# Two attention layers with spectral layers between, one core: a key tile's two half units summed one behind the other, the first sums taken from key tiles 0 and 2, and two transfers moved

## The chip, the cores and the metric

The kernel runs on one core of a Trainium2 chip. The metric is the device time of one execution in microseconds, lower is better; three runs are given with their median. A profile of one further execution, with its own time, shows what each engine of the core did: TensorE (PE; its weight loads PEld), VectorE (DVE), ScalarE (ACT), GpSimd (POOL) and SyncE (SP), which here issues transfers and passes signals on.

## The reference

Four layers in a row on x of 2048 rows and 1024 columns, each added to its input: attention, spectral filter, attention, spectral filter. The change touches the attention alone.

```python
def _A_ref(x, wqkv, wo):                       # H = 32 heads of Dh = 32
    qkv = (x @ wqkv).reshape(B, S, 3, H, Dh).transpose(2, 0, 3, 1, 4)
    q, k, v = qkv[0], qkv[1], qkv[2]
    scores = jnp.einsum("bhqd,bhkd->bhqk", q, k) * (Dh ** -0.5)
    p = _softmax(scores, axis=-1)
    o = jnp.einsum("bhqk,bhkd->bhqd", p, v)
    return o.transpose(0, 2, 1, 3).reshape(B, S, D) @ wo
...
x = x + _A_ref(_layernorm(x, axis=-1), A_wqkv, A_wo)
x = x + _B_ref(_layernorm(x, axis=-1), B_w_r, B_w_i)
x = x + _A_ref(_layernorm(x, axis=-1), A_wqkv, A_wo)
x = x + _B_ref(_layernorm(x, axis=-1), B_w_r, B_w_i)
```

## The kernel before

**Groups, chunks, steps.** An attention layer works through 8 groups of 4 heads (`g`, line 854), and in each through 4 chunks of 512 queries (`c`). A chunk meets 16 key tiles of 128 keys (`kt`). In groups 0 to 6 `chunk` (line 817) does this in eleven steps, r = 0 to 10. Steps 0 to 9 call `S3` (line 701), which makes three units of scores of 128 x 1024 each: two for one whole key tile (halves 1 and 0, two heads each: `y` and `x`) and between them one for a half unit `z`: all four heads, but only one half (256) of the queries, of a second key tile. Two steps share that second tile: steps 2i and 2i+1 make the whole tiles 3i and 3i+2 and the two half units of tile 3i+1. Step 10 calls `S` (line 720) for tile 15. Each unit lies in one of three PSUM buffers. ScalarE turns it into exponentials (`exp`, line 695) in the order y, z, x, into a buffer of the pool `at_p`, which has 8 and goes round; a buffer is free again when both its users are done, the product with V and the sum.

**The users.** `PV` (line 731) multiplies the exponentials by V on TensorE; in the even steps it takes the last two steps' three key tiles. The softmax's denominators are made by adding the exponentials of all key tiles, element by element, into `acc` on VectorE: `add` (line 746) for a whole tile's half, `add_half` (line 755) for a half unit, which touches both halves of `acc` in 256 of 512 columns. The first sums of a chunk are written by a scalar_tensor_tensor of two exponentials, in place of a sum onto `acc`: in line 760 those of tiles 0 and 1, in four pieces of 512 columns; in group 7, which has no half units, in line 750. In step r the sums are those of step r-1's units: first half 1 of the whole tile, then the half unit, then half 0 (lines 841 to 846).

**The chunk's end.** In step 0 of the next chunk `boundary` (line 809) adds tile 15; `fin` (line 765) then has TensorE sum `acc` over the keys (L768: four matmuls for four heads, two on either half of `acc`, which run side by side), and VectorE makes and applies the reciprocals. `out` (line 781) splits the result in two f16 parts in step 2 (a cast on ScalarE, a subtraction on VectorE, L785), and `store` (line 778) writes them to `od` in DRAM in step 4.

**Work beside it.** In each odd step and in step 0 `slot` (line 800) puts 12 matmuls of the next groups' q, k or v on TensorE (L427, L472), into one PSUM bank. When a q or k bank is full, ScalarE casts it and VectorE writes the rest (`split`, L215 and L216). `norms` (line 441) uses that bank too, in steps 2, 6 or 10: four matmuls (L447) and a maximum on VectorE (L449). Weights come through SyncE (L300) into three stage buffers, each of which a split frees; two splits of 512 columns are made at a time.

**Group 6 to 7.** From chunk 2, step 7 of group 6 on, `slot` has matmuls of the output projection in place of q and k (`wo_parts`, line 579; L530). They read the head outputs of groups 0 to 6, which `load_o` (line 519) brings from `od` into the space of the normalised input: `load_o(0)` for queries 0 to 511, in two pieces, `load_o(1)` for the next 512. `xres` (line 533) loads rows of the residual, `load_wo` (line 501) the projection's weights.

**Order.** In groups 0 to 6 the order of TensorE, ScalarE and SyncE is that of the program (line 853); VectorE's is chosen by the framework's planner by its own modelled times, within the dependences. SyncE has a part in `S3` (lines 710 to 714): it waits for one matmul, and TensorE waits for SyncE before the last matmuls of the step. Whatever SyncE waits for or issues in between comes ahead of that.

Of the kernel before, what the change touches and what calls it, by code (L numbers as in the profile page):

```python
# [12 lines left out]
ALU = mybir.AluOpType  # L13
# [94 lines left out]
NG, NCH, NKT, NST = 8, 4, 16, 6  # L108
# [110 lines left out]
def run(g):  # L219
    for _ in g:  # L220
        pass
# [122 lines left out]
def attention(nc, tc, layer, ap, xin, yd, wts, wo, cst, dram, flags):  # L344
# [14 lines left out]
    def bank():  # L359

        if both:
            both.append(True)
            if len(both) % 2:
                return psO.tile([128, 512], F32, name="o")
        return psX.tile([128, 512], F32, name="x")
# [75 lines left out]
    def norms(z=None):  # L441
        kind, g = ph = left_norms.pop(0)
        if g not in mx:
            mx[g] = sm.tile([128, 2], F32, name="mqk")
        z = psS.tile([128, 2, 512], F32, name="s")[:, 0] if z is None else z
        for c in range(4):
            nc.tensor.matmul(z[32 * c:32 * c + 32], cst["bones"], nrm[ph][:, c], start=True, stop=True)  # L447
        i = 0 if kind == "k" else 1
        nc.vector.reduce_max(mx[g][:, i:i + 1], z, axis=AX.X)  # L449
        if kind == "q":  # L450
            mkbias(g)
# [67 lines left out]
    def load_o(c):  # L519
        osb[c] = xhl[:, 2 + c % 2]  # L520
        for i in range(2):
            nc.sync.dma_start(osb[c][:, i, 0:7], od[i, 0:7, :, c * 512:(c + 1) * 512].rearrange("g p n -> p g n"))
# [21 lines left out]
    def wo_part(c, t, dst, nd):  # L544

        x = xres(c, t)
        st = sm.tile([128, 2, 6], F32, name="st")
        for n in range(2):
            p = bank()
            m = wo_mm(p, c, t, n, range(nd))  # L550
            for _ in range(3 * nd - 1):
                next(m)
                yield
            run(m)
            sl = slice(n * 512, n * 512 + 512)
            nc.vector.scalar_tensor_tensor(dst[:, sl], p, 1.0 / (SO * SW), x[:, sl], op0=ALU.mult, op1=ALU.add)
            if nd == 8:
                nc.vector.bn_stats(st[:, n], dst[:, sl])
                if n:
                    r0 = c * 512 + t * 128  # L560
                    nc.sync.dma_start(yd[r0:r0 + 128, :], dst)
                    nc.vector.bn_aggr(mvs[:, 8 * c + 2 * t:8 * c + 2 * t + 2], st)
            yield
# [13 lines left out]
    wo_dst = [ap.x[:, 10 + t if t in SPILL else t] for t in range(8)] + [None] * 2 + [ap.x[:, t] for t in (10, 11)]  # L577

    def wo_parts():
        load_o(0)  # L580
        load_o(1)
        for t in (2, 3, 0, 1, 4, 5, 6, 7, 8, 9, 10, 11):
            if t == 8:
                two = wvp.tile([128, 2, 1024], F32, name="wv")
                wo_dst[8], wo_dst[9] = two[:, 0], two[:, 1]
            yield from wo_part(t // 4, t % 4, wo_dst[t], 8 if t == 11 else 7)
            if t in (1, 7):
                load_o(t // 4 + 2)
# [104 lines left out]
    P, Z, O, acc = {}, {}, {}, ap.acc  # L693
# [7 lines left out]
    def S3(g, c, kt, kz, qh):  # L701

        y, z, x = (psS.tile([128, 2, 512], F32, name="s") for _ in range(3))
        zv = z.rearrange("p j (s q) -> p j s q", q=256)
        for h, i, half in RUN:
            r, (a, b) = slice(32 * h, 32 * h + 32), TERMS[i]
            o, k, q, n = ((zv[:, h % 2, h // 2], kz, c * 512 + 256 * qh, 256) if half else
                          ((x, y)[h // 2][:, h % 2], kt, c * 512, 512))
            m = nc.tensor.matmul(o, K[g][r, a, k * 128:k * 128 + 128], Q[g][r, b, q:q + n], start=i == 0, stop=i == 2).ins  # L709
            if (h, i, half) == (1, 2, 1):  # L710
                turn = nc.sync.nop(nofuse=True).ins  # L711
                tc.add_manual_dep(turn, m.name, sync, reason="the first row tiles are done with the bank")
            if (h, i, half) == (2, 0, 1):
                tc.add_manual_dep(m, turn.name, sync, reason="the last row tiles follow in the same bank")
        P[g, c, kt, 1] = exp(g, pp.tile([128, 2, 512], F32, name="p"), y)
        p = exp(g, pp.tile([128, 2, 512], F32, name="p"), z)
        Z[g, c, kz, qh] = p.rearrange("p j (s q) -> p s j q", q=256)
        P[g, c, kt, 0] = exp(g, pp.tile([128, 2, 512], F32, name="p"), x)

    def S(g, c, kt):  # L720

        s = [psS.tile([128, 2, 512], F32, name="s") for _ in range(2)]
        for i, (a, b) in enumerate(TERMS):
            for h in range(4):
                r = slice(32 * h, 32 * h + 32)
                nc.tensor.matmul(s[h // 2][:, h % 2], K[g][r, a, kt * 128:kt * 128 + 128],  # L726
                                 Q[g][r, b, c * 512:c * 512 + 512], start=i == 0, stop=i == 2)
        for hf in range(2):
            P[g, c, kt, hf] = exp(g, pp.tile([128, 2, 512], F32, name="p"), s[hf])

    def PV(g, c, kt):
        if kt == 0:
            O[g, c] = psO.tile([128, 512], F32, name="o")
        parts = [(slice(256 * q, 256 * q + 256), Z[g, c, kt, q]) for q in range(2)] if (g, c, kt, 0) in Z else \
            [(slice(0, 512), [P[g, c, kt, hf] for hf in range(2)])]
        for q, p in parts:
            for h in range(4):
                r = slice(32 * h, 32 * h + 32)
                src = p[:, h // 2, h % 2] if len(parts) == 2 else p[h // 2][:, h % 2]
                nc.tensor.matmul(O[g, c][r, q], V[g][:, kt, r], src, start=kt == 0, stop=kt == NKT - 1)  # L740
        if kt == NKT - 1:
            o = ap.oc.tile([128, 512], F32, name="oc")
            nc.scalar.copy(o, O[g, c])
            O[g, c] = o

    def add(g, c, kt, halves=(0, 1)):
        for hf in halves:
            p = P[g, c, kt, hf]
            if kt == 1:
                nc.vector.scalar_tensor_tensor(acc[:, hf], P[g, c, 0, hf], 1e-34, p, op0=ALU.add, op1=ALU.add)  # L750
            elif kt:
                last_add = nc.vector.tensor_add(acc[:, hf], acc[:, hf], p)  # L752
        return last_add if kt > 1 else None

    def add_half(g, c, kt, q):

        sl = slice(256 * q, 256 * q + 256)
        if kt == 1:
            for hf in (1, 0):
                nc.vector.scalar_tensor_tensor(acc[:, hf, :, sl], P[g, c, 0, hf][:, :, sl], 1e-34, Z[g, c, kt, q][:, hf],  # L760
                                               op0=ALU.add, op1=ALU.add)
        else:
            nc.vector.tensor_add(acc[:, :, :, sl], acc[:, :, :, sl], Z[g, c, kt, q])  # L763

    def fin(g, c, z):
        zt = on.tile([128, 16, 32], F32, name="zt")
# [26 lines left out]
    pend, done, stores = [], [], []  # L793
# [15 lines left out]
    def boundary(w):  # L809

        last_add = add(*w)
        with tc.issue_after(last_add.ins):
            wts.look()
        done.append(w[:2])
        fin(*w[:2], psS.tile([128, 2, 512], F32, name="s")[:, 0])

    def chunk(g, c):

        for r in range(11):
            i, b = divmod(r, 2)  # L820
            n = 6 * c + (r + 1) // 2
            if r < 10:
                S3(g, c, 3 * i + 2 * b, 3 * i + 1, b)
            else:
                S(g, c, 15)
            if g == c == r == 0:
                run(last_v)
            if r and not b:
                for k in range(3):
                    PV(g, c, 3 * i - 3 + k)  # L830
                    if k == 1 and r in (2, 6, 10):
                        while left_norms:
                            norms(bank())
            if r == 0 and pend:
                PV(*pend[0])
                boundary(pend.pop())
            if r == 2 and done:
                stores.append(out(*done.pop(), store=False))
            if r == 4 and stores:
                store(*stores.pop())  # L840
            if r:
                i, k = divmod(r - 1, 2)
                if r > 2:
                    add(g, c, 3 * i + 2 * k, (1,))
                add_half(g, c, 3 * i + 1, k)
                add(g, c, 3 * i + 2 * k, (0,) if r > 2 else (1, 0))
            if b or r == 0:
                slot(g, n)
            if g == NG - 2 and 4 <= n + (b or r == 0) and left and (left.pop(0) % 3 < 2):
                next(lwo)  # L850
        pend.append((g, c, 15))
# [5 lines left out]
    g = NG - 1  # L857
    with tc.manual_schedule(engines={mybir.EngineType.PE, mybir.EngineType.Activation}):
        for u in range(NCH * NKT):
            c, kt = divmod(u, NKT)  # L860
# [587 lines left out]
```

## Time and profile before

| what | us |
| --- | --- |
| median of 3 runs | 3869.43 |
| the runs | 3868.97 to 3872.74 |
| the profiled execution | 3873.68 |
| its span, first to last instruction | 3871.7 |
| TensorE busy (mean granted clock 0.99) | 3695.9 |
| VectorE busy | 3237.9 |
| ScalarE busy | 2926.3 |

In a row of the timeline stand the start and the duration in us, the engine, the line of the kernel, the operation, what it writes and reads, partitions x elements, and how many such instructions follow one another without a pause; brackets give the idle time of the engine before it and what ended that. A row of waits gives who waited for what, the total in us, how often, and the longest. A row by lines gives the busy time, the mean of one in ns, and the idle time before them. Two instructions of VectorE may overlap by some 0.08 us.

### The profile page before, as it was taken

Reading aid. Unit: us, or ns where it says so; the run is one execution under the profiler, and the core shown is the slowest. Engines: PE = TensorE matmul, PEld = TensorE weight load, DVE = VectorE, ACT = ScalarE, POOL = GpSimd, SP = SyncE. Lnnn points to the kernel's source line nnn. Section 1 sums busy time; section 2 is a strip of 40 time slices with the busy share of each in tenths; the row PEclk is TensorE's granted clock in tenths of the full one; section 3 lists DMA queues with packets and bytes.
Section 4 is the critical chain, followed back from the end, with each engine's and each line's share of the span. In section 5 each row is a group of like instructions: output and inputs, shape, how many; then the busy total and the mean of one; then the engine's idle time right before and its main releaser. Section 6 shows DMA issues by size and latency. Waiting matters only on the chain.

```text
span 3871.7 us, 90485 instructions
## 1 busy us (share of the span) xinstructions
PE 3695.9 (95%) x38871; PEld 1923.6 (50%) x38871; DVE 3237.9 (84%) x3890; ACT 2926.3 (76%) x3683; POOL 289.0 (7%) x388
## 2 busy tenths in 40 slices
PE   8999999999999899999999999999999998999998
PEld 5434544454455333368964345434543543333788
DVE  6798999899989888985658899989998998789754
ACT  5787888888888766668748888878887877666586
POOL 1000000000000000014410000000000000000143
PEclk9999999999999999999999999999999999999999
DMA  6000000000000211233150010010001102111333
GB/s 180 15 12 23 7 18 16 20 15 12 20 21 21 78 55 63 77 126 115 56 147 31 23 34 26 23 31 26 19 23 34 34 29 77 56 66 72 148 98 106
DMA packets 150156, 199.09 MB, mean 51 GB/s; under 512 B 58224, under 2 KB 104048, under 8 KB 148720
## 3 DMA queue, kind: packets, MB, share of 16 engines
q1 hardware_dynamic: 148416, 192.62, 15.5%
q8 instruction: 306, 5.01, 0.5%
q14 instruction: 106, 0.87, 0.1%
q10 hardware_dynamic: 1328, 0.59, 0.1%
HBM read 132.35 MB, written 48.23 MB: 47 GB/s over the span
## 4 chain that ended last, share of the span: by engine, by line


## 5 line engine op out<-in xcount | busy, mean ns | idle before, releaser
L696 ACT ACTIVATE p<-s,bias 128x1024 f32<-128x1024 f32 x2048 | 2138.8, 1111 | 657.0 <-PE s L709 427.9
L752 DVE TENSOR_TENSOR R<-R,p 128x1024 f32<-128x1024 f32 x1344 | 1595.5, 1220 | 105.0 <-ACT p L696 59.3
L740 PE MATMUL o<-p,R 128*32 128x512 f32 (+1 forms) x10432 | 980.5, 510 | 0.0
L427 PE MATMUL x<-big,wqk 128*128 128x512 f16 x2880 | 661.7, 380 | 16.8 <-DVE mqk L449 14.5
L709 PEld LDWEIGHTS <-R 32*128 32x128 f16 x13440 | 380.3, 92 | 503.7 <-issue 361.3
L763 DVE TENSOR_TENSOR R<-R,p 128x1024 f32<-128x1024 f32 x448 | 549.0, 1226 | 50.5 <-ACT p L696 3.5
L740 PEld LDWEIGHTS o<-p,R 128*32 128x32 f32 x10432 | 300.8, 110 | 420.2 <-issue 327.2
L427 PEld LDWEIGHTS <-wqk 128*128 128x128 f16 x3072 | 283.9, 98 | 406.3 <-issue 97.3
L709 PE MATMUL s<-R 32*128 32x512 f16 (+1 forms) x7680 | 389.1, 323 | 12.2 <-SPq L711 7.9
L472 PE MATMUL x<-wv,big 128*128 128x256 f16 x2784 | 326.7, 275 | 11.9 <-DVE mqk L449 8.0
L472 PEld LDWEIGHTS <-big 128*128 128x128 f16 x3072 | 293.5, 98 | 82.2 <-issue 40.5
L709 PE MATMUL s<-Q,R 32*128 32x512 f16 (+1 forms) x5760 | 285.6, 325 | 25.2 <-SPq L711 25.0
L530 PE MATMUL x<-big 128*128 128x512 f16 x1050 | 245.2, 384 | 11.7 <-DMA big<-od 11.7
L760 DVE SCALAR_TENSOR_TENSOR R<-p 128x512 f32<-128x512 f32 x224 | 145.3, 669 | 119.2 <-ACT p L696 119.2
L530 PEld LDWEIGHTS <-big 128*128 128x128 f16 x1344 | 125.2, 98 | 188.9 <-issue 38.6
L455 POOL PARTITION_ALL_REDUCE mall<-mqk x16 | 13.7, 855 | 2359.8 <-DVE mqk L449 2348.4
L1110 DVE TENSOR_TENSOR H<-G,H 128x512 f16<-128x512 f32 (+1 forms) x68 | 47.0, 692 | 120.2 <-ACT H L1109 120.0
L726 PE MATMUL s<-Q,R 32*128 32x512 f16 x1824 | 125.6, 377 | 2.7 <-DVE R L571 2.7
L1055 ACT COPY U<-ps 64x256 f32<-64x256 f32 (+1 forms) x272 | 97.0, 357 | 8.4 <-PE ps L1062 3.1
L726 PEld LDWEIGHTS <-R 32*128 32x128 f16 x2208 | 41.1, 92 | 124.9 <-issue 104.1
L768 PE MATMUL s<-R,ones 128*32 128x512 f32 x512 | 87.7, 609 | 14.3 <-DVE R L752 9.7
L1062 PE MATMUL ps<-cbi,H 128*128 128x256 f16 (+1 forms) x792 | 98.6, 273 | 2.8 <-ACT H L1109 1.8
(448 smaller groups left out, 3307.0 us busy)
## 6 DMA issues: line engine op xcount, KB each, us to landing
wst<-in_wp SPq DMA_DIRECT2D x96, 256.0 KB, 2.9
R<-y SPq DMA_DIRECT2D x32, 512.0 KB, 5.3
w<-in_w SPq DMA_DIRECT2D x60, 256.0 KB, 2.7
od<-ohl SPq DMA_DIRECT2D x56, 256.0 KB, 2.4
big<-od SPq DMA_DIRECT2D x16, 896.0 KB, 6.7
y<-R SPq DMA_DIRECT2D x20, 512.0 KB, 2.8
wst<-in_wo SPq DMA_DIRECT2D x32, 256.0 KB, 2.6
xres<-in_x SPq DMA_DIRECT2D x16, 512.0 KB, 3.9
```

What stands on the lines that cost most here:

```text
L427: nc.tensor.matmul(ps, a, b, start=i == 0, stop=i == 23)
L472: nc.tensor.matmul(ps[:, j], x[c][:, d, o:o + 128], w[:, n, d], start=i == 0, stop=i == 23)
L530: nc.tensor.matmul(p, a, b, start=start and d == ds[0] and i == 0, stop=stop and d == ds[-1] and i == 2)
L696: nc.scalar.activation(p, s, AF.Exp, bias=bias[g], scale=SCALE / (SQ * SQ))
L709: m = nc.tensor.matmul(o, K[g][r, a, k * 128:k * 128 + 128], Q[g][r, b, q:q + n], start=i == 0, stop=i == 2).ins
L726: nc.tensor.matmul(s[h // 2][:, h % 2], K[g][r, a, kt * 128:kt * 128 + 128], Q[g][r, b, c * 512:c * 512 + 512], start=i == 0, stop=i == 2)
L740: nc.tensor.matmul(O[g, c][r, q], V[g][:, kt, r], src, start=kt == 0, stop=kt == NKT - 1)
L752: last_add = nc.vector.tensor_add(acc[:, hf], acc[:, hf], p)
L760: nc.vector.scalar_tensor_tensor(acc[:, hf, :, sl], P[g, c, 0, hf][:, :, sl], 1e-34, Z[g, c, kt, q][:, hf], op0=ALU.add, op1=ALU.add)
L763: nc.vector.tensor_add(acc[:, :, :, sl], acc[:, :, :, sl], Z[g, c, kt, q])
L1055: nc.scalar.copy(ov[64 * r:64 * r + 64, a0:a0 + m, x], tl[64 * x:64 * x + 64, :m, r])
L1062: nc.tensor.matmul(out, l, r, start=k == 0, stop=k == len(mm_) - 1)
```

## The change

Four things change, all in `attention`.

- The order of the sums. In odd steps from 3 on only the whole tile of the step before is summed, both halves. In even steps the two half units of tile 3i-2 are summed one behind the other, then both halves of tile 3i-1. In step 1 nothing is summed.
- The first sums: tiles 0 and 2, in two instructions of 1024 columns in step 2, and tile 1's half units are then added as any other's. Group 7 keeps tiles 0 and 1.
- `store` stands in step 6 of the next chunk, not in step 4.
- `load_o(0)` stands in step 1 of chunk 2 of group 6, not at the start of `wo_parts` (step 7 of that chunk).

```diff
     def wo_parts():
-        load_o(0)
         load_o(1)
...
             p = P[g, c, kt, hf]
-            if kt == 1:
+            if kt == (1 if g == NG - 1 else 2):
                 nc.vector.scalar_tensor_tensor(acc[:, hf], P[g, c, 0, hf], 1e-34, p, op0=ALU.add, op1=ALU.add)
             elif kt:
                 last_add = nc.vector.tensor_add(acc[:, hf], acc[:, hf], p)
-        return last_add if kt > 1 else None
+        return last_add if kt > 2 else None
...
         sl = slice(256 * q, 256 * q + 256)
-        if kt == 1:
-            for hf in (1, 0):
-                nc.vector.scalar_tensor_tensor(acc[:, hf, :, sl], P[g, c, 0, hf][:, :, sl], 1e-34, Z[g, c, kt, q][:, hf],
-                                               op0=ALU.add, op1=ALU.add)
-        else:
-            nc.vector.tensor_add(acc[:, :, :, sl], acc[:, :, :, sl], Z[g, c, kt, q])
+        nc.vector.tensor_add(acc[:, :, :, sl], acc[:, :, :, sl], Z[g, c, kt, q])
...
-            if r == 4 and stores:
+            if r == 6 and stores:
                 store(*stores.pop())
-            if r:
-                i, k = divmod(r - 1, 2)
+            if b and r > 1:
+                add(g, c, 3 * i, (1, 0))
+            elif r and not b:
+                if r == 2:
+                    add(g, c, 2, (1, 0))
+                for k in range(2):
+                    add_half(g, c, 3 * i - 2, k)
                 if r > 2:
-                    add(g, c, 3 * i + 2 * k, (1,))
-                add_half(g, c, 3 * i + 1, k)
-                add(g, c, 3 * i + 2 * k, (0,) if r > 2 else (1, 0))
+                    add(g, c, 3 * i - 1, (1, 0))
+            if (g, c, r) == (NG - 2, 2, 1):
+                load_o(0)
             if b or r == 0:
                 slot(g, n)
```

## The prediction

> **What bounds the kernel now.** First the busy times in the two stretches in which the change lies, attention groups 0 to 6 of either layer (columns: PE, PEld, DVE, ACT and POOL busy, clock, DMA share, GB/s).
>
> ```profile
> 109.00:1407.00 1298.00, 1243.99 (x14570) 580.49 (x14569) 1169.12 (x1202) 1056.96 (x1164) 24.41 (x28) 0.99 0.07 22
> ...
> 2032.00:3334.00 1302.00, 1247.36 (x14586) 580.44 (x14585) 1177.09 (x1214) 1057.48 (x1164) 24.83 (x28) 0.99 0.10 32
> ```
>
> TensorE sets the end: it idles 54.0 us in the first stretch and 54.6 in the second. VectorE is busy for 1169 of 1298 us, 90%, beside it. What this change can win lies in those 109 us, and in matmuls that run slowly after a pause. So the next view is what TensorE waits for (total, times, longest).
>
> ```profile
> PE s L709 <- SPq L711: 32.9, 12, 4.2
> PE x L447 <- DVE R L216: 17.0, 6, 2.8
> PE x L427 <- DVE mqk L449: 14.5, 14, 1.3
> PE x L530 <- DMA big<-od: 11.7, 4, 4.3
> PE x L447 <- DVE Q L216: 11.5, 8, 1.6
> ...
> PE s L768 <- DVE R L752: 9.7, 8, 1.7
> ...
> PE x L472 <- DVE mqk L449: 8.0, 6, 1.6
> ...
> PE x L427 <- DVE R L216: 1.9, 6, 0.6
> ```
>
> All but the transfer are VectorE being late. L447 and L427 want a PSUM bank that a split (L216) or a maximum (L449) on VectorE has still to read. In the first row SyncE stands behind a weight load whose buffer VectorE's split has to free, and TensorE waits for the signal that SyncE passes on in every `S3`. For a sum itself (L752, L763) only `fin` (L768) waits; the sums matter because VectorE does its work in order, so whatever stands behind them comes when they are done.
>
> **The pace of the sums.** A chunk with little other work: VectorE, then TensorE and ScalarE in the same stretch.
>
> ```profile
> 440.36 1.29 DVE L760 SCALAR_TENSOR_TENSOR R<-p 128x512 f32<-128x512 f32 x2 [2.13 <-ACT p L696]
> 441.57 3.49 DVE L752 TENSOR_TENSOR R<-R,p 128x1024 f32<-128x1024 f32 x3
> ...
> 450.89 2.36 DVE L752 TENSOR_TENSOR R<-R,p 128x1024 f32<-128x1024 f32 x2
> 453.36 1.23 DVE L763 TENSOR_TENSOR R<-R,p 128x1024 f32<-128x1024 f32 x1
> 454.69 2.36 DVE L752 TENSOR_TENSOR R<-R,p 128x1024 f32<-128x1024 f32 x2
> ...
> 441.15 1.16 PE L709 MATMUL s<-Q,R 32*128 32x256 f16 x24
> ...
> 444.96 1.15 PE L709 MATMUL s<-Q,R 32*128 32x256 f16 x24
> ...
> 438.21 3.12 ACT L696 ACTIVATE p<-s,bias 128x1024 f32<-128x1024 f32 x3 [2.43 <-PE s L709]
> ```
>
> TensorE takes 444.96 - 441.15 = 3.81 a step, VectorE 454.69 - 450.89 = 3.80 for three sums: once late, it stays late. Two L752 of different halves follow at 2.36 - 1.22 = 1.14; into and out of a half unit's sum (L763), which reads both halves, the pitch is (3.80 - 1.14) / 2 = 1.33: a dependent sum costs 0.19 more. Now two steps hold two pitches of 1.14 and four of 1.33, 7.60. After the change they hold the order 3i (both halves), the two half units, 3i+2 (both halves): four of 1.14 and two of 1.33, 7.22, **0.38 less for two steps**, if the second half unit (other columns) need not wait for the first. The nearest rows: two writes to interleaved columns of one tile follow without a wait.
>
> ```profile
> 1657.57 0.68 DVE L195 TENSOR_TENSOR R<-xn 128x512 f32<-128x512 f32 x1
> 1658.17 0.69 DVE L194 TENSOR_TENSOR R<-xn 128x512 f32<-128x512 f32 x1
> ...
> L750 DVE SCALAR_TENSOR_TENSOR R<-p 128x1024 f32<-128x1024 f32 x16 | 18.8, 1218 | 0.0
> ```
>
> They start 0.60 apart with 0.68 of duration. I take no wait; the other end is 0.19 per pair of half units.
>
> **The start costs.** Four L760 (two take 1.29) become two wide ones of 1.218 (L750's row): 0.2 less work, but later. The first needs step 1's first exponential (438.21 + 1.11 = 439.32), the second its third (441.33): 441.36 to 442.59, then the half units (0.10 after it, then 1.14) to 445.07. Before, 441.57 + 3.49 = 445.06 saw one sum more done. So the new order is one pitch, **1.14, behind** after step 2; 0.76 after step 4, 0.38 after 6, level after 8, and 0.38 ahead at the last sums. The buffers of `p` are held longer: the first exponential of step 3 (445.8) takes the one that the first half unit frees at 443.9, 1.9 of cover.
>
> **The waits, by that ledger.** Rows of the kinds that count:
>
> ```profile
> 522.92 2.10 PE L768 MATMUL s<-R,ones 128*32 128x512 f32 x8 [1.41 <-DVE R L752]
> 524.95 2.76 PE L427 MATMUL x<-big,wqk 128*128 128x512 f16 x12
> ...
> 663.44 1.06 PE L768 MATMUL s<-R,ones 128*32 128x512 f32 x8
> 664.44 2.76 PE L427 MATMUL x<-big,wqk 128*128 128x512 f16 x12
> ...
> 537.21 0.68 DVE L449 TENSOR_REDUCE mqk<-x 128x1 f32<-128x512 f32 x1
> ...
> 705.06 3.12 ACT L696 ACTIVATE p<-s,bias 128x1024 f32<-128x1024 f32 x3 [2.35 <-PE s L709]
> ...
> 710.61 2.35 DVE L752 TENSOR_TENSOR R<-R,p 128x1024 f32<-128x1024 f32 x2
> 713.49 1.06 PE L768 MATMUL s<-R,ones 128*32 128x512 f32 x8
> ```
>
> `fin` takes 664.44 - 663.44 = 1.00 where the sums are in time and 2.03 where they are late (its two pairs then run one behind the other). Over one turn of two groups (eight chunks) the boundaries at 433, 477, 523 and 569 are late: four in eight, 28 in all, x -0.38 = -10.6. Where VectorE had caught up, its last sum ends at 710.61 + 2.35 = 712.96, ahead of the `fin` at 713.49. There step 9's second exponential (705.06 + 2.1 = 707.2) is now followed by its half unit, two sums, a split and the last two sums: 1.33 + 1.14 + 1.14 + 0.60 + 1.14 + 1.23, to 713.8, 0.3 past TensorE; two in eight, 14 x 0.3 = +4.2. The splits of step 10 (6 waits): -0.38 x 6 = -2.3. Those of step 6 (8 + 6 waits): +0.38 x 14 = +5.3. The maximum L449 at 537.21 came behind the sums up to the first half unit of kt 4; now behind the two wide ones, a split, two halves and one sum, from 531.66: 537.05, -0.16 x 20 = -3.2. SyncE's weight load (step 8) is level: 0. **Sum -7.** This assumes that the planner, which orders VectorE, puts the other work behind as many finished exponentials as now.
>
> **The earlier load.** Layer one, then two; last SyncE's issues.
>
> ```profile
> 1342.30 1.15 PE L709 MATMUL s<-R 32*128 32x256 f16 x24
> 1347.72 0.60 PE L530 MATMUL x<-big 128*128 128x512 f16 x2 [4.27 <-DMA big<-od]
> 1350.13 4.02 PE L530 MATMUL x<-big 128*128 128x512 f16 x9 [1.81 <-DMA big<-od]
> ...
> 1358.48 1.16 PE L709 MATMUL s<-R 32*128 32x256 f16 x24
> ...
> 1367.35 1.06 PE L768 MATMUL s<-R,ones 128*32 128x512 f32 x8
> ...
> 3269.17 1.16 PE L709 MATMUL s<-R 32*128 32x256 f16 x24
> ...
> 3280.72 1.15 PE L709 MATMUL s<-R 32*128 32x256 f16 x24
> ...
> 1342.90 4.24 SPq L522 DMA_DIRECT2D big<-od  x4
> ...
> 1347.19 2.33 SPq L539 DMA_DIRECT2D xres<-in_x  x1
> ...
> 1356.69 1.23 DVE L752 TENSOR_TENSOR R<-R,p 128x1024 f32<-128x1024 f32 x1 [6.45 <-ACT p L696]
> ...
> 1363.57 3.69 DVE L752 TENSOR_TENSOR R<-R,p 128x1024 f32<-128x1024 f32 x3
> ```
>
> Two steps took 16.18 in place of 7.62, one 11.55 in place of 3.81: 8.56 + 7.74 = 16.3 lost, gaps and slow matmuls (0.43 each at 1350.13, 0.23 at 524.95). Six steps (23 us) earlier the data is there long before: the second piece's mark came 1350.13 - 1342.90 = 7.2 after the first issue. Both ends of the copy allow it: the last reader of the space is in the chunk before, and the stores that it reads were issued a chunk earlier. SyncE's issues: four take 4.24, so two some 1 to 2, between turns 3.81 apart; at the old place the other two and `xres` (2.33) just fit, and cost up to 2 if not. The weight loads queued behind have over two steps of cover. But the pause also let VectorE catch up (6.45 idle): 1356.69 less 6.45 is 1350.24, and the chunk's rest took 1363.57 + 3.69 - 1356.69 = 10.57. Without the pause it ends at 1360.8, while `fin`, 8.56 earlier than its 1367.4, would be due at 1358.8: 2.0 late, of which the new order takes 0.4; so 1.6 of each layer goes back there, 3.2 in all. **Sum -13.** The store two steps later costs nothing: its subtraction has long finished, and the tile has a second buffer.
>
> **Rivals.** (1) *The planner packs finer*: with the sums bunched, other VectorE work slips in one sum earlier (at most 1.14 each): step 10 6.8, step 6 11, weight loads 6.8, L449 22, together 46, half of it 23: 3803 to 3826. For: a tie between a sum and a split is decided by small modelled times. Against: now a split always stands behind the third exponential's sum. (2) *The load's gain is given back* (VectorE's backlog, SyncE's issues): 3 instead of 13, and the sums 0: 3866. (3) *The pace does not rise, slower*: the second half unit waits for the first. Then two steps give 0.19, step 2 leaves 1.33, and the last sums are 0.57 late: `fin` 28 x 0.57 + 4, step 10 3.4, step 6 14 x 0.95, weight loads 6 x 0.76: +41, less 13: 3898. It decides once two steps give less than 1.14 / 4 = 0.28. Against: L194 and L195.
>
> The Trainium skill (VectorE: DVE Perf Modes, "The DRAIN you can't avoid") says that a semaphore between chained operations costs nothing extra. By that rule the pace stays, and rival 3 is dearer (1.14 late at every `fin`, some 3920). The trace disagrees, 1.33 against 1.14, so it gets 0.02 of rival 3's chance.
>
> **How the numbers follow.** The execution profiled took 3873.7 (span 3871.7), 4.3 above the median 3869.4. 3873.7 - 7 - 13 = 3853.7, at the median's level **3849**. Chances: forecast 0.50 (own range 3837 to 3861), rival 1 0.20, rival 2 0.13, rival 3 0.17. The range 3815 to 3882 leaves out the end of rival 1 and most of rival 3. A measurement tells some 0.2% (7.7 us) from no change: faster 0.68, same 0.17, slower 0.15.
>
> **What would show it.** Two L763 1.14 apart (1.33: rival 3). L530's wait for the load gone, the two steps near 3.8. The gap before step 2's sums about 2 and then 0.9. `fin` nearer 1.0 at half the boundaries. L447's longest 2.8 at 2.4, or under 1.7 for rival 1; the 4.2 of SyncE unchanged, or near 3. What makes it wrong: an exponential that waits for a sum, which no row shows now.

## The result, and the profile after

The kernel after takes 3835.39 us (median of 4 runs, 3834.0 to 3837.64) where the kernel before took 3869.2 (4 runs): a ratio of 0.9912, 95% interval 0.9895 to 0.9929, so 0.9% faster. The forecast was 3849, its range 3815 to 3882. The execution profiled took 3834.0 (span 3832.0). One of the six executions of load_alone, a run of the next section, was in a slow state (4497.39); its time there is the median of the other five.

The waits of TensorE in the profile after (who waited for what, total, times, longest; S3 is now L708, `fin` L762, whole sums L751, half units L757):

```profile
PE x L427 <- DVE mqk L449: 27.6, 14, 2.2
PE s L708 <- SPq L710: 16.1, 8, 2.5
PE x L472 <- DVE mqk L449: 13.2, 6, 2.2
...
PE s L762 <- DVE R L751: 6.3, 8, 1.4
...
PE x L447 <- DVE R L216: 5.2, 6, 0.9
...
PE x L530 <- DVE mqk L449: 2.8, 2, 1.6
...
PE x L447 <- DVE Q L216: 1.0, 6, 0.2
```

Beside the rows of before: the wait for the transfer is gone, SyncE's 32.9 has become 16.1 and the splits' 28.5 (L447) 6.2; but the maximum, 22.5 before, now costs 43.6. The gain is the small difference of two large changes, and a forecast that is near in sum can be wrong in both.

A second view puts sizes on it. The page has no table by step, so this one is worked out from the trace: from the first score matmul of a step to that of the next, added over the 56 chunks of groups 0 to 6 of both layers, in us against the kernel before. It holds the runs of the next section too. Each row is one execution, and that of the kernel before was 4.3 above its median, so one or two us in a column mean nothing.

```
                 step 0   step 3   step 6   step 7   step 8  9, 10    all
after              -4.7    +22.3    -12.3     -6.9    -16.9  -16.7  -33.0
load_alone         +0.3     -0.4     +0.8    -14.2     -1.3   -1.6  -16.8
sums_alone         -5.3    +23.8    -12.4     +5.1    -15.3  -16.8  -20.7
before_split       -1.6     -0.1    -10.1     +6.3     -9.5  -13.3  -28.5
before_max        +31.1    -18.6     +4.2     +0.1     -0.4   +2.0  +18.1
before_all        +38.8    -18.6     -4.8    -21.1    -18.3  -13.2  -36.2
mixed_split       +15.2    +19.1     -6.8     -5.3     -8.4   -4.6   +8.6
after_mixed       +21.2    +25.7     +7.7     -5.4     +7.7   +3.2  +59.7
after_max          +5.3    -18.7     -8.6    -21.2    -15.1  -16.8  -74.1
after_start       -12.6     -2.8    -14.4     -7.6    -24.3  -23.1  -85.1
```

Step 0 holds the ones sums (`fin`), steps 3 and 7 what follows a maximum, steps 6, 8, 9 and 10 what waits for a split (step 8: for SyncE, which stands behind a weight load and so behind a split). The late transfer lay in steps 7 and 8 of one chunk in each layer. Steps 1, 2, 4 and 5 are left out; "all" holds them.

VectorE's timeline shows how one kernel can lose at step 3 and win at step 6. First the start of a chunk after (start, duration; in brackets the idle time before and what ended it), then TensorE at the same place:

```profile
524.25 1.23 DVE L749 SCALAR_TENSOR_TENSOR R<-p 128x1024 f32<-128x1024 f32 x1 [1.97 <-ACT p L695]
526.26 1.23 DVE L749 SCALAR_TENSOR_TENSOR R<-p 128x1024 f32<-128x1024 f32 x1 [0.78 <-ACT p L695]
527.40 0.69 DVE L216 SCALAR_TENSOR_TENSOR R<-x,R 128x512 f16<-128x512 f32 x1
528.00 2.35 DVE L757 TENSOR_TENSOR R<-R,p 128x1024 f32<-128x1024 f32 x2
530.46 2.36 DVE L751 TENSOR_TENSOR R<-R,p 128x1024 f32<-128x1024 f32 x2
532.74 0.68 DVE L449 TENSOR_REDUCE mqk<-x 128x1 f32<-128x512 f32 x1
```

```profile
528.85 0.40 PE L447 MATMUL x<-sq,bones 128*32 128x512 bf16 x4
...
530.03 1.24 PE L708 MATMUL s<-R 32*128 32x256 f16 x24
533.48 0.81 PE L427 MATMUL x<-big,wqk 128*128 128x512 f16 x3 [2.21 <-DVE mqk L449]
```

The two half units take 2.35 together, so they start 2.35 - 1.22 = 1.13 apart: the second does not wait for the first. But VectorE idles 1.97 and 0.78 before the two wide first sums, and the maximum, whose four matmuls are done at 529.3, stands behind two half units and both sums of key tile 3. TensorE waits 2.21 for it, where the kernel before waited 1.27 at the same place:

```profile
537.95 2.75 PE L427 MATMUL x<-big,wqk 128*128 128x512 f16 x12 [1.27 <-DVE mqk L449]
```

A later stretch of a chunk after shows the pace and the split's place:

```profile
674.37 4.63 DVE L751 TENSOR_TENSOR R<-R,p 128x1024 f32<-128x1024 f32 x4
679.03 2.36 DVE L757 TENSOR_TENSOR R<-R,p 128x1024 f32<-128x1024 f32 x2
681.43 1.23 DVE L751 TENSOR_TENSOR R<-R,p 128x1024 f32<-128x1024 f32 x1
682.57 0.68 DVE L216 SCALAR_TENSOR_TENSOR R<-x,R 128x512 f16<-128x512 f32 x1
```

Two steps' sums take 681.43 - 674.37 = 7.06, against 7.60 before; and the split stands behind the first half's sum of its step, ahead of the second's. The kernel before in the same chunk:

```profile
687.54 1.23 DVE L763 TENSOR_TENSOR R<-R,p 128x1024 f32<-128x1024 f32 x1
688.87 1.23 DVE L752 TENSOR_TENSOR R<-R,p 128x1024 f32<-128x1024 f32 x1
690.01 0.68 DVE L216 SCALAR_TENSOR_TENSOR R<-x,R 128x512 f16<-128x512 f32 x1
```

Here the split stands behind the second half's sum (688.87) as well: in the kernel after the planner has put it one sum earlier.

### The profile page after: what moved, and what is told of

The parts are those of the page before. It is cut to its first block, busy times and chain, and to the rows that moved or that the text cites. A ratio compares the mean times of both kernels' runs of the same rounds, so it can differ in the third digit from the quotient of the medians.

```text
span 3832.0 us, 89965 instructions
## 1 busy us (share of the span) xinstructions
PE 3694.9 (96%) x38871; PEld 1924.6 (50%) x38871; DVE 3222.6 (84%) x3778; ACT 2927.7 (76%) x3683; POOL 289.3 (8%) x388
## 4 chain that ended last, share of the span: by engine, by line
## 5 line engine op out<-in xcount | busy, mean ns | idle before, releaser
L751 DVE TENSOR_TENSOR R<-R,p 128x1024 f32<-128x1024 f32 x1232 | 1450.2, 1220 | 76.0 <-ACT p L695 54.3
L427 PE MATMUL x<-big,wqk 128*128 128x512 f16 x2880 | 668.7, 383 | 28.1 <-DVE mqk L449 27.6
L757 DVE TENSOR_TENSOR R<-R,p 128x1024 f32<-128x1024 f32 x560 | 666.3, 1221 | 31.8 <-ACT p L695 25.2
L708 PEld LDWEIGHTS <-R 32*128 32x128 f16 x13440 | 379.6, 92 | 487.9 <-issue 364.9
L708 PE MATMUL s<-R 32*128 32x512 f16 (+1 forms) x7680 | 389.7, 323 | 7.7 <-ACT p L695 5.3
L708 PE MATMUL s<-Q,R 32*128 32x256 f16 (+1 forms) x5760 | 282.8, 323 | 14.9 <-SPq L710 14.7
L749 DVE SCALAR_TENSOR_TENSOR R<-p 128x1024 f32<-128x1024 f32 x128 | 156.1, 1225 | 158.6 <-ACT p L695 158.6
L530 PE MATMUL x<-big 128*128 128x512 f16 x1050 | 240.8, 380 | 2.8 <-DVE mqk L449 2.8
L530 PEld LDWEIGHTS <-big 128*128 128x128 f16 x1344 | 124.8, 98 | 176.8 <-issue 38.0
L1054 ACT COPY B<-ps 64x256 f32<-64x256 f32 (+1 forms) x272 | 97.2, 357 | 5.5 <-PE ps L1061 1.7
L762 PE MATMUL s<-R,ones 128*32 128x512 f32 x512 | 91.8, 603 | 9.1 <-DVE R L751 6.3
```

What stands on the lines that cost most here:

```text
L427: nc.tensor.matmul(ps, a, b, start=i == 0, stop=i == 23)
L530: nc.tensor.matmul(p, a, b, start=start and d == ds[0] and i == 0, stop=stop and d == ds[-1] and i == 2)
L762: nc.tensor.matmul(z[32 * h:32 * h + 32], cst["ones"], acc[:, h // 2, h % 2], start=True, stop=True)
L1054: nc.scalar.copy(ov[64 * r:64 * r + 64, a0:a0 + m, x], tl[64 * x:64 * x + 64, :m, r])
```

## The experiments

All times are medians; "before" is the kernel before run beside them on the same chip (3867.8 to 3869.2 in the three groups). The names of the lines are those of each run's own text and shift by one or a few.

**The two parts apart.** load_alone is the kernel before with this edit; sums_alone is the kernel after without it.

```diff
     def wo_parts():
-        load_o(0)
         load_o(1)
...
+            if (g, c, r) == (NG - 2, 2, 1):
+                load_o(0)
             if b or r == 0:
                 slot(g, n)
```

> The kernel before with one part of the change: the first copy back of head outputs six steps earlier. VectorE's order is that of the kernel before. By the prediction's sum: 8.56 + 7.74 won in the two late steps, 3.2 given back at the sums' end: 13 less than before, some 3856. Rival (the gain is given back, VectorE being late there in any case): 3 less, 3866. In the trace: no wait of L530 for the transfer in either case; what tells them apart is the wait of the next ones sums and of the splits in the same chunk.

> The kernel after with the copy back where it was before; VectorE's order is that of the kernel after. By the prediction's ledger the new sums give 7 less than before, 3862. By the two traces (splits of steps 6, 8 and 10 come one sum earlier and are worth far more than the pace, the maximum costs more): 34 less in all, of which the load is 13, so 21 less, 3848.

Measured: load_alone 3854.71 (ratio 0.9968, 0.9955 to 0.9981), 13.1 less than before; sums_alone 3849.18 (0.9950, 0.9936 to 0.9964), 18.6 less. Together 31.7, and the kernel after is 33.8 below: the parts add up within what the intervals leave open. The net is as forecast, 13, but its two terms were both smaller: steps 7 and 8 of the two chunks with the transfer became 14.4 shorter, not 16.3, and 1.5 of it was given back, not 3.2. In place of the two waits of L530 for the transfer, 4.27 and 1.81 before, TensorE now has none (the 1.32 is the maximum):

```profile
1343.58 2.53 PE L530 MATMUL x<-big 128*128 128x512 f16 x11 [1.32 <-DVE mqk L449]
...
1350.93 2.33 PE L530 MATMUL x<-big 128*128 128x512 f16 x10
```

What is given back stands at the `fin` behind that chunk (VectorE, then TensorE):

```profile
1355.83 3.68 DVE L751 TENSOR_TENSOR R<-R,p 128x1024 f32<-128x1024 f32 x3
```

```profile
1358.71 1.90 PE L767 MATMUL s<-R,ones 128*32 128x512 f32 x8
1360.55 2.55 PE L530 MATMUL x<-big 128*128 128x512 f16 x11
```

The last sum ends at 1359.51, behind the start of `fin`, which takes 1360.55 - 1358.71 = 1.84 in place of 1.00. Layer two loses 0.63 there. In the table this is hidden: step 0 is only +0.3, because other boundaries, far from the transfer, came out shorter in that execution.

For the sums the forecast was 7, outside the interval of 18.6 (14 to 25): the order, not the load, is what has to be explained.

**The place of the splits, in the old order.** One edge for the order of VectorE: the last sum of an even step is issued behind the latest split.

```diff
-    return high, nc.vector.scalar_tensor_tensor(lo, src, scale, hi, op0=ALU.mult, op1=ALU.subtract)
+    split.low = nc.vector.scalar_tensor_tensor(lo, src, scale, hi, op0=ALU.mult, op1=ALU.subtract)
+    return high, split.low
...
-                add(g, c, 3 * i + 2 * k, (0,) if r > 2 else (1, 0))
+                with tc.issue_after(split.low.ins) if r > 2 and k else nullcontext():
+                    add(g, c, 3 * i + 2 * k, (0,) if r > 2 else (1, 0))
```

> The kernel before, its sums in their old order and at their old pace, only that the last sum of an even step is issued behind the latest split: every split of steps 4 to 10 stands one sum earlier, where the kernel after has it. If it is the place of the splits that pays: each wait shorter by one dependent sum, 1.33: L447 28.5 to some 11, SyncE's 32.9 to some 22, those of step 10 shorter as much, and fewer slow matmuls behind them: 25 to 40 less than before, 3829 to 3844. Rival (it is the pace of the new sums that pays, place alone nothing): within 5 of before, 3864 to 3870.

Measured: 3841.12, ratio 0.9926 (0.9913 to 0.9940), 26.7 less than before. No sum is in another order than before, and the waits shrink as the kernel after's do:

```profile
PE x L428 <- DVE mqk L450: 21.2, 14, 1.9
PE s L710 <- SPq L712: 17.1, 8, 3.0
...
PE x L448 <- DVE R L216: 8.3, 6, 1.4
```

SyncE's wait falls from 32.9 to 17.1, and that for the first kind of split from 17.0 to 8.3, their longest by 1.2 and 1.4: one dependent sum. The wait for the maximum grows beside them, from 14.5 to 21.2 in the first row (step 7 +6.3). So the place of a split alone is worth 27, more than the whole new order won by itself (18.6).

**The pace, with the place held.** In mixed_split the pairs of the kernel after are undone within their step, and the splits held where the kernel after has them; in after_mixed the planner is left to place them.

```diff
                 for k in range(2):
                     add_half(g, c, 3 * i - 2, k)
-                if r > 2:
-                    add(g, c, 3 * i - 1, (1, 0))
+                    if r > 2:
+                        with tc.issue_after(split.low.ins) if k else nullcontext():
+                            add(g, c, 3 * i - 1, (1 - k,))
```

> The kernel after, but an even step's half units and its third tile's sums alternate again (half unit, half, half unit, half), so that two steps hold four dependent pitches, not two; every split and maximum is held at the place that it has in the kernel after. This leaves the pace alone. By the prediction's 0.19 for a dependent pitch two steps take 0.38 more: step 6 waits 14 x 0.76, the weight loads 8 x 1.14, step 10 and the ones sums up to 1.5 each where they are late now: 20 to 45 more than the kernel after, 3855 to 3880. Rival (the pace does not matter, only places do): within 5 of the kernel after, 3830 to 3840.

> As the run mixed_split, but the splits left to the planner, which puts them one sum later, where the kernel before has them. What it takes over mixed_split is the price of the place in the new order: 25 to 30 if it is what before_split won in the old order; nothing if the place only mattered there.

Measured: mixed_split 3881.33, ratio 1.0036 (1.0023 to 1.0050), 45.9 more than the kernel after: the pace matters, at the upper end of what was expected. Its VectorE, and then the waits:

```profile
589.67 1.22 DVE L758 TENSOR_TENSOR R<-R,p 128x1024 f32<-128x1024 f32 x1
591.00 1.23 DVE L752 TENSOR_TENSOR R<-R,p 128x1024 f32<-128x1024 f32 x1
592.33 1.23 DVE L758 TENSOR_TENSOR R<-R,p 128x1024 f32<-128x1024 f32 x1
593.66 3.50 DVE L752 TENSOR_TENSOR R<-R,p 128x1024 f32<-128x1024 f32 x3
597.19 1.23 DVE L758 TENSOR_TENSOR R<-R,p 128x1024 f32<-128x1024 f32 x1
```

```profile
PE x L428 <- DVE mqk L450: 27.6, 14, 2.2
PE s L709 <- SPq L711: 23.5, 10, 3.4
PE s L763 <- DVE R L752: 19.1, 13, 2.8
...
PE x L448 <- DVE R L216: 13.1, 6, 2.5
```

Two steps take 597.19 - 589.67 = 7.52 in place of 7.06, and the waits that come late in a chunk grow (ones sums 6.3 to 19.1, SyncE 16.1 to 23.5, L447's counterpart 5.2 to 13.1), while the maximum, early in the chunk, stays at 27.6. That is what a slower pace must look like; the splits and maxima stand behind as many sums of their steps as in the kernel after.

after_mixed took 3931.89, ratio 1.0164 (1.0150 to 1.0178): 50.6 over mixed_split, though 25 to 30 was expected. A split's place costs more in an order that is already behind: step 6 alone loses 14.5 and step 8 16.1 between the two rows of the table. So there is no one price of a place.

**The maximum's place.** The sums of the step behind a maximum are issued behind it; after_max is the kernel after with this, before_max the kernel before with its like.

```diff
-        nc.vector.reduce_max(mx[g][:, i:i + 1], z, axis=AX.X)
+        flags["top"] = nc.vector.reduce_max(mx[g][:, i:i + 1], z, axis=AX.X)
...
             if b and r > 1:
-                add(g, c, 3 * i, (1, 0))
+                with tc.issue_after(flags.pop("top").ins) if "top" in flags else nullcontext():
+                    add(g, c, 3 * i, (1, 0))
```

> The kernel after, only that the sums of the step behind a maximum (L449) are issued behind it. If the maximum's place behind two more sums is what TensorE waits for: its 27.6 + 13.2 + 2.8 go to under 5, with the slow matmuls behind them: 45 to 55 less than the kernel after, 3780 to 3790. Rival (the sums, 0.6 to 1.2 later, are late next, so the wait moves to the splits and to the ones sums): some 10 less than the kernel after, 3825.

> The kernel before, each maximum ahead of the sums of the step behind it. Its waits for maxima, 22.5, go; if the old pace (3.80 for 3.81) lets nothing be caught up, the sums, later by the maximum, come late to the splits and the ones sums, and some is given back: 10 to 20 less than before, 3848 to 3858. Rival (all of it is won, and the slow matmuls too): 25 or more less, 3842 or under.

Measured: after_max 3792.0, ratio 0.9803 (0.9789 to 0.9816), 43.4 less than the kernel after. before_max 3889.59, ratio 1.0058 (1.0044 to 1.0072): the same edit in the old order makes it 20.4 **slower**, which neither theory had. Step 3 wins the same 18.6 against the kernel before in both, but before_max loses 31.1 in step 0. The rows of `fin` at one boundary, before_max first (VectorE's last sums, then TensorE), then the kernel before:

```profile
757.45 3.69 DVE L752 TENSOR_TENSOR R<-R,p 128x1024 f32<-128x1024 f32 x3
```

```profile
760.15 2.10 PE L768 MATMUL s<-R,ones 128*32 128x512 f32 x8 [0.92 <-ACT p L696]
762.18 1.48 PE L472 MATMUL x<-wv,big 128*128 128x256 f16 x12
```

```profile
758.56 1.07 PE L768 MATMUL s<-R,ones 128*32 128x512 f32 x8
759.56 1.70 PE L472 MATMUL x<-wv,big 128*128 128x256 f16 x14
```

In before_max the last sum ends at 757.45 + 3.69 = 761.14, behind the start of `fin`; TensorE waits 0.92, then its two pairs run one behind the other, 2.03 in place of 1.00. The bracket names an exponential, the second of three, which ended at 760.07; but the kernel before starts `fin` when the first has ended, so what it waited for must be the sum of tile 15's first half, which ended at 760.01. The step that was 5.21 at the maximum is now 3.89, 1.32 won; this boundary gives back 0.92 + 1.03 = 1.95. The other boundaries agree: of the 14 chunks whose step 3 waited for a maximum, 12 are now followed by a step 0 that is 1.7 to 2.1 longer. TensorE's pauses were what let VectorE, at 3.80 for TensorE's 3.81, finish in time. Taken away early in the chunk they come back, dearer, at its end. In the new order VectorE gains 7.62 - 7.06 = 0.56 on TensorE in every two steps, so the maximum's pause can go: after_max wins 55 over the kernel after in steps 3 and 7 and gives back 10 in step 0.

**The old order with everything else.** before_all has the edits of before_split, before_max and load_alone together.

> The old order of the sums with all that has been tried beside it: the splits one sum earlier, each maximum ahead of the sums of the step behind, and the first copy back early. If these add up: 27 (before_split) + 12 (load_alone) + some 25 (the 28.8 that before_split waits for maxima): 3804. What is left between it and after_max, 3792, is the new order of the sums by itself. Rival (they do not add up, the sums being late in any case): over 3815.

Measured: 3836.55, ratio 0.9919 (0.9906 to 0.9933), so 31.5 less than before where their sum would have been 27 + 13 - 20 = 20 and the expectation said 64. The rival held: they do not add up, step 0 taking 38.8. after_max, with the maxima and the load in the same way and the splits at the same place, is 44.6 below it: that is what the new order of the sums, dear start and all, brings beside those edits.

**The start of a chunk.** after_start is the kernel after with the first sums of the kernel before, tiles 0 and 1.

```diff
-            if kt == (1 if g == NG - 1 else 2):
+            if kt == 1:
...
+            elif r == 1:
+                add_half(g, c, 1, 0)
+            elif r == 2:
+                add_half(g, c, 1, 1)
+                add(g, c, 2, (1, 0))
             elif r and not b:
-                if r == 2:
-                    add(g, c, 2, (1, 0))
                 for k in range(2):
                     add_half(g, c, 3 * i - 2, k)
```

(`add_half` has its four narrow first sums back.)

> The kernel after, but a chunk's sums begin with tiles 0 and 1 again (four narrow first sums, two of them in step 1), then tile 2 and tile 3; from step 4 on the order is that of the kernel after. If the start with tiles 0 and 2 is what makes the maximum later than before (2.2 in place of 1.3) and leaves VectorE behind for the steps that follow: the maxima wait 0.9 less, 20 x 0.9 and the slow matmuls behind them, and SyncE's and the ones sums' waits shrink too: 20 to 40 less than the kernel after, 3795 to 3815. Rival (the start costs nothing, only the maximum's place in the order does, which stays): within 5 of the kernel after, 3830 to 3840.

Measured: 3781.96, ratio 0.9777 (0.9764 to 0.9790): 53.4 less than the kernel after, more than was expected. So this part of the change, beside the other parts, costs more than the whole change brings. The same chunk as in the rows of after:

```profile
518.45 1.29 DVE L759 SCALAR_TENSOR_TENSOR R<-p 128x512 f32<-128x512 f32 x2 [2.10 <-ACT p L695]
519.66 1.22 DVE L751 TENSOR_TENSOR R<-R,p 128x1024 f32<-128x1024 f32 x1
520.79 0.69 DVE L216 SCALAR_TENSOR_TENSOR R<-x,R 128x512 f16<-128x512 f32 x1
521.39 3.49 DVE L751 TENSOR_TENSOR R<-R,p 128x1024 f32<-128x1024 f32 x3
524.80 0.68 DVE L449 TENSOR_REDUCE mqk<-x 128x1 f32<-128x512 f32 x1
```

```profile
523.23 1.24 PE L708 MATMUL s<-R 32*128 32x256 f16 x24
525.53 2.75 PE L427 MATMUL x<-big,wqk 128*128 128x512 f16 x12 [1.07 <-DVE mqk L449]
```

The idle 0.78 between the first sums is gone, the sums of tiles 0 to 3 stand ahead of the maximum as in the kernel after, and TensorE's pause is 1.07 for 2.21: 1.14 less, one sum.

**The store.** store_back is the kernel after with `store` at step 4 again (`r == 4` for `r == 6`).

> The kernel after with the store of a head output two steps earlier again, at step 4; VectorE's order is the same. If the store costs nothing at either place: within 5 of the kernel after, 3830 to 3840. Rival (the subtraction ends later in the new order, SyncE stands before the store and the weight loads behind it): over 3840, with SyncE's waits over 16.1.

Measured: 3835.76, ratio 0.9915 (0.9901 to 0.9928), SyncE's wait 16.1 as in the kernel after. The store's place costs nothing.

**Versions that beat both kernels.** best is after_max with both sums of an even step's third tile behind the split, so that each split stands two sums earlier than in the kernel before; best_start has the start of after_start as well.

> after_max, and both sums of an even step's third tile issued behind the latest split, so that the splits come one sum earlier again. The 16.1 of SyncE, the 9.6 of L447 and those of step 10 shrink by up to 1.14 each: 10 to 20 less than after_max, 3772 to 3782. Rival (the sums, later by a split, or a split that waits for its matmuls, make the ones sums late): 3792 or more.

> The run best, with a chunk's sums beginning with tiles 0 and 1 as in after_start. What best still waits for VectorE is 11.0 of the ones sums and 6.3 of SyncE; if the start leaves VectorE behind, half or more of it goes: 8 to 15 less than best, 3760 to 3767. Rival (the 0.2 of work that the narrow first sums add counts, 56 x 0.2): 3775 to 3785.

Measured: best 3775.42, ratio 0.9763 (0.9749 to 0.9776); best_start 3765.12, ratio 0.9731 (0.9718 to 0.9744), the fastest of all, 104 below the kernel before. What TensorE still waits for VectorE in the attention of best_start is little; the largest rows:

```profile
PE s L768 <- DVE R L752: 7.6, 6, 2.1
PE s L709 <- SPq L711: 5.4, 6, 0.9
```

The start is worth 10.3 there, not 53: once splits and maxima stand early, little waits for the sums that it delays.

## Why the prediction was near, point by point

**What bounds the kernel** held: the waits that changed in the two stretches are for VectorE, but for the transfer's.

**The pace** had the mechanism right and the size low. The second half unit waits for nothing, as taken. But a dependent pitch is not always 1.33. In the rows of after, four sums take 679.03 - 674.37 = 4.66, which is three pitches of 1.14 and one of 1.24; the two half units take 2.40, 1.14 and one of 1.26. So a dependent sum costs some 0.11 there, not 0.19, and two steps save 0.54, not 0.38. In the trace before, each half unit's sum had a semaphore instruction of its own ahead of it (224 of them in the first layer's stretch 109 to 1407), each waiting for the sum ahead of it, while the exponential was a second thing to wait for; after, all but two of 280 have none there, the exponential being a step old. That 1.33 goes with the extra instruction and 1.25 with its absence is seen wherever a half unit's sum and a whole one follow each other (before: all with it, 1.32 to 1.33; after: 375 without it, 1.25, and 54 with it, 1.32; mixed_split has both kinds too); it was not tried by itself. What the pace is worth, 46 with the places held, is far more than the ledger gave it. Of it, by the table, 20 lie in step 0, 5.5 in step 6, 8.5 in step 8 and 12 in steps 9 and 10, so it looks as if VectorE's lateness is handed on from wait to wait through the chunk; no run shows this by itself.

**The start costs** had the right size, 1.14 (2.21 less 1.07), and the wrong consequence. The ledger let it shrink by 0.38 for every two steps and so charged little for it; after_start shows 53 (and 10 where splits and maxima stand early).

**The maximum** is the first step that failed: it was put behind "a split, two halves and one sum", -0.16 each and -3.2 in all. It stood behind two sums, one more, and so 0.94 later than before (2.21 for 1.27). With its slow matmuls, steps 3 and 7 of sums_alone lost 28.9.

**The splits** are the second, and the sum's largest error: "This assumes that the planner, which orders VectorE, puts the other work behind as many finished exponentials as now." It did not: with the two half units first, a split came ahead of the second half's sum. +5.3 for step 6, 0 for step 8 and -2.3 for step 10 were forecast, +3 together; sums_alone shows -12.4, -15.3 and -16.8 (steps 9 and 10), -44.5. That is the mechanism of the first rival, though half of it only, since that rival let the maxima come earlier too, and they came later.

**The ones sums**, -10.6 + 4.2 = -6.4, came to -5.3 in step 0 of sums_alone.

**The earlier load** was 13 by the sum and 13.1 by measurement, with both terms too large: 14.4 won for 16.3, 1.5 given back for 3.2. That fits the sum's mechanism, VectorE losing its pause, and not the second rival, where all but 3 is given back. **The store** was 0 and 0.

So -7 for the sums was -18.6, an error of +32 (maxima) against one of -47 (splits). That the two nearly cancel is luck, and with it the nearness of the forecast. The total lies just below the forecast's own range, 3837 to 3861, towards the first rival, whose 3803 to 3826 it misses too. The third rival's mechanism (no faster pace) was refuted by the trace; but an order that gains as little, mixed_split (0.08 for two steps, where that rival had 0.19), did take 3881, slower than before, even with the splits at their early place; the rival's 3898 was not far off.

The Trainium skill (VectorE: DVE Perf Modes, "The DRAIN you can't avoid") says that a semaphore between chained operations costs nothing extra. Here the pitches are 1.14 without a wait for the sum ahead, about 1.25 and 1.33 with one, and an order with two more of the dear ones in two steps costs 46 us: the measurement decides.

## What to carry to other kernels

When the engine that follows (VectorE at 3.80) has the pace of the one that sets the end (TensorE at 3.81), savings of waits need not add up: a pause taken away at one place comes back at the next, and can come back dearer, as in before_max. Give the follower some reserve first, here by placing independent instructions side by side; then the same edit pays. And where a planner orders an engine, work out from the new durations where the urgent small work (a maximum, a split) will stand, as closely as the pace of the bulk: one place in the order was worth 27 here in the old order and 51 in mixed_split's, where the whole change brought 34.

## What the runs showed of the hardware that was not expected

The same pause can be followed by slow matmuls or not. Two windows of 3.5 us behind a pause for the maximum, of 2.20 and 2.21 (busy times of PE, PEld, DVE, ACT and POOL, then the granted clock):

```profile
899.60:903.10 3.50, 3.46 (x10) 1.29 (x10) 3.47 (x4) 0.60 (x1) 0.00 (x0) 0.61 0.00 0
533.40:536.90 3.50, 3.42 (x30) 1.63 (x33) 3.47 (x5) 0.63 (x1) 0.00 (x0) 1.00 0.00 0
```

```profile
533.48 2.75 PE L427 MATMUL x<-big,wqk 128*128 128x512 f16 x12 [2.21 <-DVE mqk L449]
...
899.64 4.44 PE L427 MATMUL x<-big,wqk 128*128 128x512 f16 x12 [2.20 <-DVE mqk L449]
```

Twelve matmuls take 2.75 at a clock of 1.00 and 4.44 at 0.61, so the pause ahead of 899.64 costs 1.7 more than it lasts. The clock falls behind the pause, not in it: the first four of the slow twelve still start 0.22 apart, from the fifth on 0.43. Of the 14 steps 3 with this pause in both layers 8 last 6.1 and 6 last 7.5 to 7.8. The Trainium skill (TensorE: Matmul & The Clock Gate, "Part 1: The HAM clock gate (the "warmup" mystery)") says that the clock is halved after an idle window of some 3.4 us and that the window runs freely. That equal pauses end differently agrees with a window that runs freely; but a pause of 2.2, shorter than the page's window, was followed by slow matmuls here in 6 cases of 14. What told those 6 from the other 8 was not tried.
